# Row maxima in visits of seven, four banks to one reduction: an attention and MLP kernel on one core

## The chip, the core and the metric

The kernel runs on one core of a Trainium2 chip. The core has a matrix engine (TensorE, PE in the profile; its weight loads are PEld), a vector engine (VectorE, DVE), a scalar engine (ScalarE, ACT) and a general one (GpSimd, POOL). SyncE (SP) issues most of the transfers. Matmuls write to PSUM, which has eight banks of 512 fp32 columns by 128 partitions. The metric is the device time of one execution in microseconds.

## The reference

A token mixer with a gate: attention over 2048 tokens and a token-wise MLP on the same input, mixed by a sigmoid.

```
x = A_x                                  # 1 x 2048 x 448, fp32
g = sigmoid((x * gate_w).sum(-1))
q, k, v = split(x @ wqkv)                # 16 heads of 28
p = softmax(q k^T * 28**-0.5)
a = (p v) @ wo
y = layernorm(x)
b = gelu(y @ w1 + b1) @ w2 + b2          # 448 -> 1792 -> 448
out = g * a + (1 - g) * b
```

All of it is fp32. The kernel splits each operand of a product into a high and a low part and adds three products (high by high, high by low, low by high).

## The kernel before

The work runs in three stretches.

**Projections** (start to about 114 us). q, k and v of four chunks of 512 tokens are computed. q and k go out to DRAM (qk), v through three staging tiles `vt` to DRAM (vs). Each chunk has seven tiles of q and k and then four of v; a list `ahead`/`behind` with 44 steps (`at(step, ...)`) hangs loads, layer-norm statistics and the first weights of the MLP into this order. The pools of this stretch lie in SBUF where the MLP's tiles lie later: w2, then `hh` and `hl` in falling order of f. In the pool `qw` the tiles stand in this order: wh, wl, wv, then `vt`, then small ones, so that `vt` lies under `hh` and `hl` of f = 0 to 2.

**MLP** (about 114 to 467 us). Four chunks c, each with two phases. In the first, `mlp1(c, f)` runs 11 full-array matmuls for each of 14 blocks f into a PSUM bank, and ScalarE takes gelu of it twice (into `hh`, rounded, and `h`), GpSimd makes `hl`, the rest. In the second, `mlp2(c, i)` accumulates one of four token tiles i over the 14 blocks, three matmuls for each f, and ScalarE copies the sum out (`gb`). Both take banks 0 and 1 in turn, the very last tile bank 7. During the first chunk the weights w1 and w2 are still being loaded through staging tiles (s, lnr, more) and split.

**Attention** (about 467 us to the end). Scores of 16 pairs of four heads and 512 queries, exponentials on ScalarE, then products with v into bank 7. The softmax needs the maximum of each row of scores ahead of time, and these maxima are computed by extra matmuls of 28 rows, with one reduction on VectorE for each 512 keys.

**Row maxima.** This is what the change is about. `RowMax` holds 16 sets (four groups of heads by four query chunks) of 64 products each. A product is a 28-row matmul in one of the four row groups j of TensorE (line 440), for a query tile i and a key chunk k, into a bank; VectorE reduces it to one column of `mx` (lines 420 and 422). A 65th place per set, `close`, transposes the finished maxima (line 406). The next product is taken from the row group with most left, so that row groups follow each other 0, 1, 2, 3.

The sets are spread by `Filler` as filling work. In the MLP, `filler.run` is called after each matmul of the first phase and at two places for each f of the second. It counts `slot` up by the weight of that matmul and, once six products are due (MG), issues a visit of six on banks 2 to 7. Of the 1040 places 480 (MLP_MAX) are planned in the MLP; the remainder go singly into the attention loop, up to three at each group of five score units. When all are done the attention loop goes into a late mode with seven units to a group.

In `issue`, products that are held are reduced two banks at a time where the columns of `mx` allow; column (j * 4 + i) * 4 + k puts row groups 16 apart, and the pair is cut where j wraps from 3 to 0.

The order of each engine's work is written out by hand (`manual_schedule`), so instructions run in program order on each engine, and each waits by semaphores for what it needs.

Of the kernel before, what the change touches and what calls it, by code (L numbers as in the profile page):

```python
# [7 lines left out]
F32 = mybir.dt.float32  # L8
F32R = mybir.dt.float32r
AF = mybir.ActivationFunctionType  # L10
OP = mybir.AluOpType
AX = mybir.AxisListType.X
# [3 lines left out]
P = 128  # L16
S = 2048
D = 448
H = 16
# [6 lines left out]
TPC = CH // P  # L26
NF = F // P
NM = 2 * D // P
EPS = 1e-5
SCALE = DH ** -0.5  # L30
MLP_MAX = 480
MLP_G = MLP_MAX // 260
MG = 6
FS = 4
WARM = 10
W1, W2 = 0.233, 0.205
LINE = 16
LQ = 12
STEPS = (2, 5, 7, 8, 9, 10)
# [4 lines left out]
def kernel(ctx: ExitStack, tc: tile.TileContext, xt, wqk, wv, wo, xk, w1, b1, w2, b2,  # L44
                          ident_d, sel_d, out):
    nc = tc.nc
# [6 lines left out]
    eps_t = const.tile([P, 1], F32, name="eps_t")  # L53
# [22 lines left out]
    bank = ctx.enter_context(tc.tile_pool(name="pbank", bufs=1, space=PSUM)).tile([P, 8, CH], F32, name="bank")  # L76
# [80 lines left out]
    with tc.tile_pool(name="qx", bufs=2) as qx, tc.tile_pool(name="qo", bufs=4) as qo, \  # L157
# [11 lines left out]
        def spare(i):  # L169

            return mw1.tile([P, 2, CH], F32, name=f"w1f{i}")

        wh = qw.tile([P, NM, 4, P], F32R, name="wh")
        wl = qw.tile([P, NM, 4, P], F32R, name="wl")
        wt = {}
# [7 lines left out]
            nc.gpsimd.tensor_sub(wl[:, m], wt[m], wh[:, m].bitcast(F32))  # L183

        wvh, wvl = (qw.tile([P, 4, CH], F32R, name=f"wv{x}")[:, :, :450] for x in "hl")
        vt = [qw.tile([P, H, 32], F32, name=f"vt{i}") for i in range(3)]

        xh, xl = {}, {}
        xraw = {}
# [109 lines left out]
        banks = [next_ps() for m in range(NM)]  # L299
# [41 lines left out]
        def at(n, what, *args, to=behind):  # L341
            to[n].append((what, args))
# [13 lines left out]
        at(22, ln_turn, 0, TPC)  # L356
        at(24, ln_load, 0, to=ahead)
        at(28, ln_rows, TPC, NT)
        at(37, ln_turn, TPC, NT)
        for t, (f, x) in enumerate(((24, 27), (25, 28), (31, 34), (32, 35))):  # L360
            at(f, ln_fetch, 0, t, to=ahead)
# [19 lines left out]
    class RowMax:  # L381
# [27 lines left out]
            nc.vector.tensor_scalar(mt, ps[:4 * TPC, :P], -1.0, None, op0=OP.mult)  # L409
            self.queue.dma_start(ms[g][:, c * CH:(c + 1) * CH].rearrange("j (i x) -> j i x", x=P), mt.bitcast(F32))  # L410

        def issue(self, first, n, rows=None):

            held = []

            def reduce():
                if held:
                    (b0, c0), (b1, c1) = held[0], held[-1]
                    if b0 == b1:
                        nc.vector.reduce_max(self.mx[:, c0:c0 + 1], bank[:, b0], axis=AX)  # L420
                    else:
                        nc.vector.reduce_max(self.mx[:, c0:c1 + 1:c1 - c0], bank[:, b0:b1 + 1], axis=AX)  # L422
                    held.clear()

            for b in range(first, first + n):
                if self.done >= NG * NC * 65:
                    break
                self.done += 1
                left = sum(len(x) for x in self.left)
                if self.last is not None and (left <= 56 or self.n == NG * NC):  # L430
                    reduce()
                    self.close(bank[:, b])
                    continue
                most = max(range(4), key=lambda j: (len(self.left[j]), -j))
                j = max(rows, key=lambda j: len(self.left[j])) if rows else most
                if not self.left[j]:
                    j = most
                i, k = self.left[j].pop(0)
                r = slice(32 * j, 32 * j + DH)
                nc.tensor.matmul(bank[:, b], self.qds[self.n][r, i * P:(i + 1) * P],  # L440
                                 khi[self.n // NC][r, k * 512:(k + 1) * 512], start=True, stop=True)
                at = (j * TPC + i) * 4 + k
                if held and held[0][1] > at:
                    reduce()
                held.append((b, at))
                if len(held) == 2:
                    reduce()
                if left == 41 and self.n + 1 < NG * NC:
                    self.load(self.n + 1)
                g, c = divmod(self.n, NC)  # L450
                if c == NC - 1 and g < MLP_G and all(n != k for x in self.left for _, n in x):
                    load_khr(g + 1, k)
                if left == 1:
                    reduce()
                    self.last = mpool.tile([P, 4 * TPC], F32, name="mf")
                    nc.vector.reduce_max(self.last, self.mx.rearrange("p (a k) -> p a k", k=4), axis=AX)
                    if self.n + 1 < NG * NC:
                        self.begin(self.n + 1)
                    else:
                        self.n += 1  # L460
                        self.left = [[]] * 4
            reduce()

    class Filler:


        def __init__(self):
            self.max = None
            self.first = self.upto = self.slot = 0
            self.slots = 1  # L470

        @property
        def done(self):
# [10 lines left out]
            left = self.upto - self.done  # L484
            return left if self.slot >= self.slots else min(left, int(due))

        def run(self, n=1):


            if self.max is not None and self.due(n) >= min(MG, self.upto - self.done) > 0:  # L490
                self.max.issue(2, min(MG, self.upto - self.done))

    filler = Filler()

# [48 lines left out]
    def load_qm(n):  # L543

        while filler.done < min(65 * NG * NC, 65 * (n + 1) + 9):
            filler.max.issue(5, 1)
        g, c = divmod(n, NC)
        nc.sync.dma_start(qs[n][0][DH:P:32].bitcast(F32), ms[g][:, c * CH:(c + 1) * CH])

# [4 lines left out]
    def scores(units, most, tiles, between=None):  # L554

        def product(p, i):
            u = units[p]
            n, k, j = u // 4 // NT, u // 4 % NT, u % 4  # L560
            g, (qh, ql) = n // NC, qs[n]
            a, b, r = ((khi[g], qh, DH + 1), (klo[g], qh, DH), (khi[g], ql, DH))[i]
            r = slice(32 * j, 32 * j + r)
            nc.tensor.matmul(bank[:, p], a[r, k * P:(k + 1) * P], b[r], start=(i == 0), stop=(i == 2))  # L564

        def exps(at):
            t = tiles(len(at), at[0])
            nc.scalar.activation(t, bank[:, at[0]:at[-1] + 1], AF.Exp, scale=SCALE)  # L568
            for i, p in enumerate(at):
                probs[units[p]] = t[:, i]  # L570

        ua = len(units) - UA if len(units) > U else UA
        first, last = list(range(len(units)))[:ua], list(range(len(units)))[ua:]
        if most > 0:
            filler.max.issue(5, 1, [(units[0] + 3) % 4])
        for i in range(3):
            for p in first:
                product(p, i)
        exps(first)
        if between:  # L580
            between()
        for i in range(3):
            for p in last:
                product(p, i)
            if i == 0 and most > 1:
                filler.max.issue(6, 1, [(units[0] + 1) % 4, (units[0] + 2) % 4])
        if last:
            exps(last)
        if most > 2:
            filler.max.issue(5, 1, [(units[0] + 1) % 4, (units[0] + 2) % 4])  # L590


    ml = ExitStack()
# [7 lines left out]
    more = [mh.tile([P, CH], F32, name=f"more{i}") for i in range(2)]  # L601
# [4 lines left out]

    def mlp1(c, f):

        ps = bank[:, f % 2]
        ops = []  # L610
        for t in range(3):
            ops += [(w1h[f][:, t], yh[:, t]), (w1h[f][:, t], yl[:, t]), (w1l[f][:, t], yh[:, t])]
        ops += [(w1h[f][:, 3], yh[:, 3]), (w1l[f][:, 3], yh[:, 3])]
        for i, (a, b) in enumerate(ops):
            nc.tensor.matmul(ps, a, b, start=(i == 0), stop=(i == len(ops) - 1))  # L615
            filler.run(W1 if c else 0.65 * W1)
        h = mh.tile([P, CH], F32, name="h", bufs=2)
        nc.scalar.activation(hh[f], ps, AF.Gelu_apprx_tanh, bias=b1s[:, f:f + 1])  # L618
        nc.scalar.activation(h, ps, AF.Gelu_apprx_tanh, bias=b1s[:, f:f + 1])  # L619
        nc.gpsimd.tensor_sub(hl[f], h, hh[f].bitcast(F32))  # L620

    def mlp2(c, i):

        sl = slice(i * P, (i + 1) * P)
        last = c * TPC + i == NT - 1
        a = bank[:, 7 if last else i % 2, :D]
        for f in range(NF):
            nc.tensor.matmul(a, hh[f][:, sl], w2h[f], start=(f == 0), stop=False)  # L628
            nc.tensor.matmul(a, hh[f][:, sl], w2l[f], start=False, stop=False)  # L629
            rows = not last and (c * TPC + i < NT - 2 or f < 10) and (c + i > 0 or f > 3)  # L630
            if rows:
                filler.run(2 * W2)
            nc.tensor.matmul(a, hl[f][:, sl], w2h[f], start=False, stop=(f == NF - 1))  # L633
            if rows:
                filler.run(W2)
            if last and f == NF // 3:
                scores(list(range(U)), 0, early)
        gb = mh.tile([P, CH], F32, name="h", bufs=2)[:, :D]
        nc.scalar.activation(gb, a, AF.Copy)  # L639
        nc.sync.dma_start(gbs[c * TPC + i], gb)  # L640
# [199 lines left out]
    with tc.manual_schedule(engines=ENGINES):  # L840
# [3 lines left out]
        at = -1  # L844
# [124 lines left out]
```

## Time and profile before

| | |
|---|---|
| median of 3 runs | 1114.16 us (1113.55 to 1114.87) |
| the profiled execution | 1113.87 us, span 1112.1 us |
| TensorE busy | 1103.7 us (99%), 8156 matmuls, granted clock 1.000 |
| VectorE busy | 739.5 us (66%) |
| ScalarE busy | 634.4 us (57%) |
| GpSimd busy | 330.2 us (30%) |
| row-maxima reductions | 620 of one bank at 687 ns, 202 of two banks at 1219 ns |

A row of the timeline gives start, duration, engine, line, operation, what it writes and reads, and a count where like rows were merged; in square brackets stands idle time ahead of it and what ended that. Matmuls are pipelined: their rows overlap, so the distance from start to start is the time that one costs. A row of the windows view gives the stretch, its length, and busy time and count for each engine, then the granted clock, the share of the DMA engines and their GB/s. A group's row gives engine, operation, tiles, shapes and count, then busy time and mean, then idle time of the engine ahead of the group.

### The profile page before, as it was taken

To read this page: it belongs to the slowest core of one execution; us is meant where nothing else is said; L and a number is where in the kernel's file an instruction comes from. 1 tells how busy PE (TensorE), PEld (TensorE's weight loads), DVE (VectorE), ACT (ScalarE), POOL (GpSimd) and SP (SyncE) were. 2 spreads that over 40 slices of the span, in tenths; PEclk is the share of its full clock that TensorE was granted. 3 is DMA by queue.
4 is the path that set the end of the run, shared out by engine and by line. 5 is a ranking of instruction groups with operands and counts; after the bars stand their busy time and mean duration, and the time that the engine had idled before them with its cause. 6 is when DMAs were issued, how large, how long until landed. Compare 5 with 4: busy or idle time off the path is not lost.

```text
span 1112.1 us, 19809 instructions
## 1 busy us (share of the span) xinstructions
PE 1103.7 (99%) x8156; PEld 674.0 (61%) x8156; DVE 739.5 (66%) x1033; ACT 634.4 (57%) x660; POOL 330.2 (30%) x352
## 2 busy tenths in 40 slices
PE   9999999999999999999999999999999999999998
PEld 7888777777767767744444444444444444454546
DVE  3553488888888889576666676666667767747103
ACT  5434640331230231287877887887878878747572
POOL 5015564242334331013112221320223024343250
PEclk9999999999999999999999999999999999999999
DMA  7987641011111022162100220012011003002011
GB/s 258 356 272 277 178 125 49 9 47 39 47 55 37 25 65 75 49 165 74 28 19 20 61 73 20 20 28 52 27 58 37 18 20 94 12 26 69 35 53 59
DMA packets 53079, 84.35 MB, mean 76 GB/s; under 512 B 8516, under 2 KB 28500, under 8 KB 52076
## 3 DMA queue, kind: packets, MB, share of 16 engines
q1 hardware_dynamic: 48732, 76.27, 21.6%
q0 software_dynamic: 4256, 6.81, 2.3%
q8 instruction: 64, 1.05, 0.4%
q14 instruction: 27, 0.22, 0.1%
HBM read 56.40 MB, written 26.49 MB: 75 GB/s over the span
## 4 chain that ended last, share of the span: by engine, by line
PE 97%; DMA 1%; DVE 1%; ACT 1%; issue 0%; SPq 0%; ACTq 0%
PE bank L835 22%; PE bank L564 20%; PE bank L440 16%; PE bank L615 13%; PE bank L220 5%; PE bank L633 5%; PE bank L628 4%; PE bank L629 4%; PE bank L232 3%; PE bank L322 1%; PE bank L738 1%; PE bank L739 1%; PE bank L740 1%; DMA raw<-in_xt 1%; DMA vs<-vt 1%; DVE mx L420 0%
## 5 line engine op out<-in xcount | busy, mean ns | idle before, releaser
L568 ACT ACTIVATE pt<-bank 128x1536 f32<-128x1536 f32 (+1 forms) x387 | 461.5, 1243 | 122.0 <-PE bank L564 122.0
L420 DVE TENSOR_REDUCE mx<-bank 128x1 f32<-128x512 f32 x620 | 411.0, 687 | 173.6 <-PE bank L440 158.9
L835 PE MATMUL bank<-pt,vg 128*32 128x512 f32 x1948 | 260.4, 602 | 0.0
L422 DVE TENSOR_REDUCE mx<-bank 128x2 f32<-128x1024 f32 x202 | 237.7, 1219 | 32.0 <-PE bank L440 31.8
L440 PE MATMUL bank<-khi,qd 28*128 28x512 f32 x512 | 242.4, 480 | 0.3 <-DVE mx L420 0.2
L440 PEld LDWEIGHTS bank<-khi,qd 28*128 28x128 f32 x512 | 92.5, 181 | 150.1 <-DVE mx L420 107.8
L564 PE MATMUL bank<-qh,klo 28*128 28x512 f32 x1024 | 174.2, 392 | 0.0
L564 PE MATMUL bank<-qh,khi 29*128 29x512 f32 x768 | 156.4, 480 | 0.8 <-ACT khi L568 0.5
L615 PE MATMUL bank<-y,w1f 128*128 128x512 f32 x616 | 152.9, 398 | 0.3 <-ACT h L619 0.2
L615 PEld LDWEIGHTS bank<-y,w1f 128*128 128x128 f32 x616 | 112.4, 188 | 34.9 <-issue 11.8
L564 PE MATMUL bank<-ql,khi 28*128 28x512 f32 x768 | 129.9, 391 | 0.0
L620 POOL TENSOR_TENSOR hl<-h,hh 128x512 fp32r<-128x512 f32 x56 | 72.3, 1291 | 120.9 <-ACT h L619 74.0
L618 ACT ACTIVATE hh<-bank,b1s 128x512 fp32r<-128x512 f32 x56 | 38.5, 687 | 97.9 <-PE bank L615 96.2
L835 PEld LDWEIGHTS bank<-pt,vg 128*32 128x32 f32 x1948 | 44.6, 108 | 77.2 <-issue 76.8
L564 PEld LDWEIGHTS bank<-qh,klo 28*128 28x128 f32 x1024 | 87.4, 185 | 3.6
L756 POOL DMA_DIRECT2D lt<-ob x15 | 10.9, 724 | 255.7 <-DVE ob L755 255.7
L639 ACT ACTIVATE h<-bank 128x448 f32<-128x448 f32 x16 | 8.7, 544 | 135.1 <-PE bank L633 101.0
L564 PEld LDWEIGHTS bank<-qh,khi 29*128 29x128 f32 x768 | 60.9, 182 | 39.2 <-ACT pt L568 24.5
L633 PE MATMUL bank<-w2h,hl 128*128 128x448 f32 x224 | 84.6, 378 | 0.0
L628 PE MATMUL bank<-w2h,hh 128*128 128x448 f32 x224 | 83.1, 371 | 0.7 <-DVE mx L420 0.7
L629 PE MATMUL bank<-w2l,hh 128*128 128x448 f32 x224 | 81.4, 363 | 0.0
L440 PE MATMUL bank<-khr,qd 28*128 28x512 f32 x512 | 79.9, 466 | 0.0
(137 smaller groups left out, 1286.4 us busy)
## 6 DMA issues: line engine op xcount, KB each, us to landing
qk<-hl SPq DMA_DIRECT2D x28, 512.0 KB
raw<-in_xt SPq DMA_DIRECT2D x16, 256.0 KB
vs<-vt SPq DMA_DIRECT2D x16, 256.0 KB
s<-in_xt SPq DMA_DIRECT2D x16, 256.0 KB
rc<-rls POOLq DMA_DIRECT2D x60, 64.0 KB, 2.2
w1f<-in_xk SPq DMA_DIRECT2D x8, 448.0 KB
gbs<-h SPq DMA_DIRECT2D x16, 224.0 KB
klo<-qk SPq DMA_DIRECT2D x16, 224.0 KB
```

The source lines that it names most:

```text
L220: nc.tensor.matmul(ps, a, b, start=(i == 0), stop=(i == len(ops) - 1))
L420: nc.vector.reduce_max(self.mx[:, c0:c0 + 1], bank[:, b0], axis=AX)
L422: nc.vector.reduce_max(self.mx[:, c0:c1 + 1:c1 - c0], bank[:, b0:b1 + 1], axis=AX)
L440: nc.tensor.matmul(bank[:, b], self.qds[self.n][r, i * P:(i + 1) * P], khi[self.n // NC][r, k * 512:(k + 1) * 512], start=True, stop=True)
L564: nc.tensor.matmul(bank[:, p], a[r, k * P:(k + 1) * P], b[r], start=(i == 0), stop=(i == 2))
L568: nc.scalar.activation(t, bank[:, at[0]:at[-1] + 1], AF.Exp, scale=SCALE)
L615: nc.tensor.matmul(ps, a, b, start=(i == 0), stop=(i == len(ops) - 1))
L620: nc.gpsimd.tensor_sub(hl[f], h, hh[f].bitcast(F32))
L628: nc.tensor.matmul(a, hh[f][:, sl], w2h[f], start=(f == 0), stop=False)
L629: nc.tensor.matmul(a, hh[f][:, sl], w2l[f], start=False, stop=False)
L633: nc.tensor.matmul(a, hl[f][:, sl], w2h[f], start=False, stop=(f == NF - 1))
L835: nc.tensor.matmul(pv[32 * j:32 * j + 32, :], vg[n // NC][:, k, 32 * j:32 * j + 32], probs.pop(4 * step + j), start=(k == 0), stop=(k == N ...
```

## The change

Six edits:

- The accumulators of both MLP phases alternate between banks 0 and 7 in place of 0 and 1. Visits in the first phase use banks 1 to 6.
- In the second phase, for f from 2 to 9, a visit takes seven banks: 1 to 6 and whichever of 0 and 7 is not the accumulator of this tile. Outside these f, a visit has six and waits until eight products are due.
- `mx` has its columns in the order (k, i, j), so successive products are neighbours, and `reduce` joins held banks into one instruction where bank and column both go up by one, cut ahead of the fifth bank of the visit. A new rule, `clear`, holds the next visit until as many slots have gone by as the reductions of the last are reckoned to take (0.57 for each bank, less 0.5). The closing reduction of a set reads `mx` with a stride.
- MLP_MAX goes from 480 to 484; MG is dropped.
- A one-element gelu at step 30 of the projections loads ScalarE's table there.
- `vt` is allocated ahead of wh and wl, so it lies under `hh` and `hl` of the last f.

```diff
-MLP_MAX = 480
+MLP_MAX = 484
-MG = 6
+RED = 0.57
+        vt = [qw.tile([P, H, 32], F32, name=f"vt{i}") for i in range(3)]
         wh = qw.tile([P, NM, 4, P], F32R, name="wh")
...
-        vt = [qw.tile([P, H, 32], F32, name=f"vt{i}") for i in range(3)]
...
+        at(30, nc.scalar.activation, qw.tile([P, 1], F32, name="table"), eps_t, AF.Gelu_apprx_tanh)
...
             def reduce():
-                if held:
-                    (b0, c0), (b1, c1) = held[0], held[-1]
-                    if b0 == b1:
-                        nc.vector.reduce_max(self.mx[:, c0:c0 + 1], bank[:, b0], axis=AX)
-                    else:
-                        nc.vector.reduce_max(self.mx[:, c0:c1 + 1:c1 - c0], bank[:, b0:b1 + 1], axis=AX)
-                    held.clear()
+                while held:
+                    n = 1
+                    b, at = held[0]
+                    while n < len(held) and held[n] == (b + n, at + n) and held[n][0] not in banks[4:5]:
+                        n += 1
+                    nc.vector.reduce_max(self.mx[:, at:at + n], bank[:, b:b + n] if n > 1 else bank[:, b], axis=AX)
+                    del held[:n]
...
-                at = (j * TPC + i) * 4 + k
-                if held and held[0][1] > at:
-                    reduce()
-                held.append((b, at))
-                if len(held) == 2:
-                    reduce()
+                held.append((b, (k * TPC + i) * 4 + j))
...
-                    nc.vector.reduce_max(self.last, self.mx.rearrange("p (a k) -> p a k", k=4), axis=AX)
+                    nc.vector.reduce_max(self.last.rearrange("p (j i) -> p j i", j=4),
+                                         self.mx.rearrange("p (k i j) -> p j i k", k=4, j=4), axis=AX)
...
-        def run(self, n=1):
-            if self.max is not None and self.due(n) >= min(MG, self.upto - self.done) > 0:
-                self.max.issue(2, min(MG, self.upto - self.done))
+        def run(self, n=1, banks=(), wait=0):
+            if self.max is not None:
+                wait = 0 if banks else wait
+                banks = (banks or [1, 2, 3, 4, 5, 6])[:self.upto - self.done]
+                if self.due(n) >= min(len(banks) + wait, self.upto - self.done) > 0 and self.slot >= self.clear:
+                    self.max.issue(banks)
+                    self.clear = self.slot + len(banks) * RED - 0.5
...
-        ps = bank[:, f % 2]
+        ps = bank[:, 7 * (f % 2)]
...
-        a = bank[:, 7 if last else i % 2, :D]
+        a = bank[:, 7 * (i % 2), :D]
...
+            more = ([0, 1, 2, 3, 4, 5, 6] if i % 2 else [7, 1, 2, 3, 4, 5, 6]) if 2 <= f < NF - 4 else ()
             rows = not last and (c * TPC + i < NT - 2 or f < 10) and (c + i > 0 or f > 3)
             if rows:
-                filler.run(2 * W2)
+                filler.run(2 * W2, more, 2)
             nc.tensor.matmul(a, hl[f][:, sl], w2h[f], start=False, stop=(f == NF - 1))
             if rows:
-                filler.run(W2)
+                filler.run(W2, more, 2)
```

In the attention loop the calls `issue(5, 1, ...)` and `issue(6, 1, ...)` become `issue([5], ...)` and `issue([6], ...)`, with the same effect.

More of the change, by code (lines that the diff above doesn't have):

```diff
@@ L410, in close, with issue @@
             self.queue.dma_start(ms[g][:, c * CH:(c + 1) * CH].rearrange("j (i x) -> j i x", x=P), mt.bitcast(F32))
-        def issue(self, first, n, rows=None):
+        def issue(self, banks, rows=None):
             held = []
             def reduce():
-                if held:
-                    (b0, c0), (b1, c1) = held[0], held[-1]
-                    if b0 == b1:
-                        nc.vector.reduce_max(self.mx[:, c0:c0 + 1], bank[:, b0], axis=AX)
-                    else:
-                        nc.vector.reduce_max(self.mx[:, c0:c1 + 1:c1 - c0], bank[:, b0:b1 + 1], axis=AX)
-                    held.clear()
-            for b in range(first, first + n):
+                while held:
[5 more added lines that the diff above has]
+                    del held[:n]
+            for b in banks:
                 if self.done >= NG * NC * 65:
@@ L470, in __init__ @@
             self.slots = 1
+            self.clear = 0
         @property
@@ L545, in load_qm @@
         while filler.done < min(65 * NG * NC, 65 * (n + 1) + 9):
-            filler.max.issue(5, 1)
+            filler.max.issue([5])
         g, c = divmod(n, NC)
@@ L574, in scores @@
         if most > 0:
-            filler.max.issue(5, 1, [(units[0] + 3) % 4])
+            filler.max.issue([5], [(units[0] + 3) % 4])
         for i in range(3):
@@ L585, in scores @@
             if i == 0 and most > 1:
-                filler.max.issue(6, 1, [(units[0] + 1) % 4, (units[0] + 2) % 4])
+                filler.max.issue([6], [(units[0] + 1) % 4, (units[0] + 2) % 4])
         if last:
@@ L589, in scores @@
         if most > 2:
-            filler.max.issue(5, 1, [(units[0] + 1) % 4, (units[0] + 2) % 4])
+            filler.max.issue([5], [(units[0] + 1) % 4, (units[0] + 2) % 4])
     ml = ExitStack()
```

## The prediction

> **What bounds the kernel now.** I read the page first, then the chain that ended last, then TensorE's timeline inside single stages, and last VectorE and ScalarE beside it.
>
> ```profile
> PE 1103.7 (99%) x8156; PEld 674.0 (61%) x8156; DVE 739.5 (66%) x1033; ACT 634.4 (57%) x660; POOL 330.2 (30%) x352
> PEclk9999999999999999999999999999999999999999
> PE 97%; DMA 1%; DVE 1%; ACT 1%; issue 0%; SPq 0%; ACTq 0%
> L420 DVE TENSOR_REDUCE mx<-bank 128x1 f32<-128x512 f32 x620 | 411.0, 687 | 173.6 <-PE bank L440 158.9
> L422 DVE TENSOR_REDUCE mx<-bank 128x2 f32<-128x1024 f32 x202 | 237.7, 1219 | 32.0 <-PE bank L440 31.8
> ```
>
> TensorE is busy 99% of the span at full clock, and 97% of the chain is TensorE. So a change gains only what it takes out of TensorE's stream, or out of the few holes in it. The change works on the visits of the row maxima (line 440) inside the mlp stages. A visit is a handful of 28-row matmuls put between full-array ones. The second mlp phase has these (its four turns, in order; the last column pairs are matmul records of line 440):
>
> ```profile
> 154.40:197.60 43.20, 7.53 (x59) 3.41 (x59) 1.00 0.18 60
> 243.20:287.40 44.20, 8.39 (x65) 4.13 (x65) 1.00 0.12 40
> 332.50:376.60 44.10, 8.37 (x65) 4.03 (x65) 1.00 0.10 34
> 423.10:467.30 44.20, 6.19 (x47) 2.86 (x47) 1.00 0.11 37
> ```
>
> 59 + 65 + 65 + 47 = 236. Stepping the due rule of Filler.run through the loops gives 40 visits of six there (10, 11, 11, 8), or 240 places, four of which are the transposes of close. So code and trace agree, and the same stepping can be trusted for the changed rule.
>
> What does one visit cost? One piece of the second mlp phase, and the undisturbed pace at its end:
>
> ```profile
> 246.27 0.73 PE L440 MATMUL bank<-khr,qd 28*128 28x512 f32 x6
> 246.93 0.47 PE L633 MATMUL bank<-w2h,hl 128*128 128x448 f32 x1
> ...
> 250.16 0.73 PE L440 MATMUL bank<-khr,qd 28*128 28x512 f32 x6
> ...
> 456.95 0.47 PE L628 MATMUL bank<-w2h,hh 128*128 128x448 f32 x1 [0.72 <-DVE mx L420]
> 457.26 0.36 PE L629 MATMUL bank<-w2l,hh 128*128 128x448 f32 x1
> ...
> 459.88 0.37 PE L633 MATMUL bank<-w2h,hl 128*128 128x448 f32 x1
> ```
>
> From 457.26 to 459.88 lie 13 steps, so a full matmul takes 2.62 / 13 = 0.2015 us. From visit to visit (246.27 to 250.16, 3.89 us) lie 15 of them, 3.02 us. A visit of six costs 0.87 us of TensorE: two rounds (four row groups at once, then two) and the change of form on both sides. In the first phase:
>
> ```profile
> 114.31 5.19 PE L615 MATMUL bank<-y,w1f 128*128 128x512 f32 x22
> ...
> 301.49 0.82 PE L440 MATMUL bank<-khr,qd 28*128 28x512 f32 x6
> 302.24 3.21 PE L615 MATMUL bank<-y,w1f 128*128 128x512 f32 x13
> 305.38 0.73 PE L440 MATMUL bank<-khr,qd 28*128 28x512 f32 x6
> ```
>
> 22 in 5.19 us with the last 0.39 long give 0.2286 us each; 3.89 - 13 x 0.2286 = 0.92 us per visit.
>
> **Fewer visits.** Stepping the new rule (484 planned; seven in f 2 to 9, six elsewhere, wait 2 outside, clear) gives 41 visits of six in the first phase (was 40) and in the second 20 of seven and 16 of six (was 40 of six). That is 77 for 80; 482 of the 484 are issued and two slip into attention, because clear forbids one more call. Seven matmuls cycle over four row groups, so they still take two rounds, the second with three. That a second round of three starts together is seen in a score group:
>
> ```profile
> 1046.23 0.50 PE L564 MATMUL bank<-qh,khi 29*128 29x512 f32 x3
> 1046.57 0.39 PE L564 MATMUL bank<-qh,klo 28*128 28x512 f32 x3
> ```
>
> So the seventh is free, and the sum is -4 x 0.87 + 0.92 = **-2.6 us**. Bounds: -3.5 (the extra first-phase visit hidden in a hole) and +4.2 (each seventh opens a round of 1046.57 - 1046.23 = 0.34 us, 20 x 0.34 = 6.8). I take -2.6, nearest to the row just shown. Against it speaks a rule of the Trainium skill ("TensorE: Matmul & The Clock Gate", Part 3, the cost of the per-tile semaphore tail): semaphore increments of packed matmuls come one after the other, 26.3 ns each beside 4.7 ns per tile. By that page a seventh counting matmul would add, as an estimate, 31 ns to a visit, 20 x 31 ns = 0.6 us, and the whole sum below would be -3.2. No row here has seven, so the trace cannot yet say.
>
> **Reductions, and the banks they free.** Nothing of the kernel before shows three or four banks in one instruction. The two groups above give 1219 - 687 = 532 ns per further bank, so about 1.75 us for three and 2.28 for four. Back to back they overlap:
>
> ```profile
> 246.81 3.49 DVE L422 TENSOR_REDUCE mx<-bank 128x2 f32<-128x1024 f32 x3 [0.67 <-PE bank L440]
> 250.70 3.49 DVE L422 TENSOR_REDUCE mx<-bank 128x2 f32<-128x1024 f32 x3 [0.41 <-PE bank L440]
> ```
>
> Three pairs take 3.49, not 3.66: 0.08 saved per joint. The first starts 0.54 us after the visit. Before: the last pair is done 0.54 + 3.49 = 4.03 us after the visit, and the fifth matmul of the next visit, the first to need it, comes at 3.89 + 0.34 = 4.23. Margin 0.20. After, six as 4 + 2: 3.42, margin 0.27. Seven as 4 + 3 (odd tiles): 3.95; as 1 + 3 + 3 (even tiles, because bank 7 and bank 1 are not neighbours): 4.02, done at 4.56. The next visit after seven comes 18 matmuls on, 18 x 0.2015 + 0.87 = 4.50, its second round at 4.84. Margin 0.28. So no visit waits longer than now, and VectorE keeps its idle 0.4 us per visit. I book 0, bounds -1.5 (the small waits of visits beside a close go) and +2 (0.1 us in each of the 20 visits of seven). What was late next to DVE is the other accumulator: a visit of seven needs it copied out.
>
> ```profile
> 175.62 0.47 PE L633 MATMUL bank<-w2h,hl 128*128 128x448 f32 x1
> ...
> 176.19 0.54 ACT L639 ACTIVATE h<-bank 128x448 f32<-128x448 f32 x1 [10.02 <-PE bank L633]
> ```
>
> The copy is over 1.1 us after the last matmul of a tile; the earliest visit of seven (f = 2) comes eight matmuls, 1.6 us, later. Free.
>
> **The hole ahead of the last tile.** Now bank 7 is both a filler bank and the accumulator of the last tile. The last visit is at 452.81:
>
> ```profile
> 452.81 0.79 PE L440 MATMUL bank<-khr,qd 28*128 28x512 f32 x6
> ...
> 455.86 0.37 PE L633 MATMUL bank<-w2h,hl 128*128 128x448 f32 x1
> ...
> 456.21 0.68 DVE L420 TENSOR_REDUCE mx<-bank 128x1 f32<-128x512 f32 x1
> ```
>
> Bank 7 is reduced last (456.21 + 0.68 = 456.89), and the tile starts at 456.95. Its second matmul is at 457.26 where the pace gives 455.86 + 2 x 0.2015 = 456.26: a hole of 1.00 us. After the change the last visit is in tile 14 at f = 9 as well, but on banks 7, 1 to 6 with bank 7 reduced first, alone: free 0.54 + 0.69 = 1.23 us after the visit, with 13 matmuls (2.6 us) between. **-1.0 us**; bounds -1.0 and 0 (if something unseen holds the tile). The scores at f = 4 need banks 0 to 4, reduced by then (4.56 us against 13 + 14 matmuls, 5.4 us).
>
> **Gelu table and vt.** The third and fourth mlp1 rounds now start late:
>
> ```profile
> 117.08 1.28 ACT L618 ACT_TABLE_LOAD   x1 [1.98 <-PE bank L615]
> 118.37 0.69 ACT L618 ACTIVATE hh<-bank,b1s 128x512 fp32r<-128x512 f32 x1
> 118.96 0.68 ACT L619 ACTIVATE h<-bank,b1s 128x512 f32<-128x512 f32 x1
> 121.29 0.69 ACT L618 ACTIVATE hh<-bank,b1s 128x512 fp32r<-128x512 f32 x1 [1.65 <-DMA vs<-vt]
> ...
> 122.75 0.63 ACT L105 ACTIVATE w1f<-more 128x512 fp32r<-128x512 f32 x1 [0.19 <-DMA more<-in_w]
> ...
> 124.32 0.68 ACT L619 ACTIVATE h<-bank,b1s 128x512 f32<-128x512 f32 x1
> ...
> 119.69 3.65 PE L615 MATMUL bank<-y,w1f 128*128 128x512 f32 x13 [0.19 <-ACT h L619]
> ...
> 122.61 7.60 PE bank L615 x32
> 121.00:124.00 3.00, 2.87 (x13) 2.07 (x12) 0.59 (x1) 2.52 (x5) 1.31 (x2) 1.00 0.96 319
> ```
>
> Round 2 starts at 119.69 for 114.31 + 22 x 0.2286 = 119.34, round 3 at 122.61 for 119.69 + 2.51 = 122.20: 0.76 us lost. Both causes go: the table is loaded some 30 us earlier, where ScalarE has holes, and vt no longer lies under hh and hl of f = 0 to 2. But the next thing is late at once. ScalarE converts w1f from more before round 2's gelu, and that waits for its transfer, which lands just before 122.75 with the DMA engines 96% busy. So h of round 2 stays at 125.00, and round 4, which needs it, starts there instead of at about 125.2. **-0.15 us**, bounds 0 (the transfer lands even later) and -0.8 (it lands a microsecond earlier). The table's cover upstream:
>
> ```profile
> 90.33 0.60 ACT L208 ACTIVATE hl<-bank 128x512 fp32r<-128x512 f32 x1 [1.94 <-PE bank L220]
> ```
>
> 1.28 + 0.2 fit into idle stretches like this one's 1.94 us; without them TensorE would still have eight banks in turn. vt's new place lies under hh of the last f, written 30 us later. Its transfers and their order on SP's queue stay, as do the khr loads on POOL's.
>
> **Attention.** Two row maxima fewer there; stepping its loop gives 186 calls with three and none with two (was one), and 200 calls in all either way, so late mode starts one call sooner. **-0.1 us**, bounds -0.5 and +0.3 (late calls cut TensorE's stream once more). The strided read of mx at the end of a set stays one small instruction: 0.
>
> **Sum**: -2.6 - 1.0 - 0.15 - 0.1 = -3.85 us. The profiled execution took 1113.87 us, its span 1112.1; it would be 1110.0. The median of the runs, 1114.16, lies 0.3 above it: 1110.3.
>
> **Rivals.**
> *VectorE becomes the bound (slower).* If a four-bank instruction ran like four singles, 4 x 0.687 = 2.75 us, it would end 0.47 later; a visit of six then waits 0.47 - 0.27 = 0.20, one of seven (4 + 3, 0.78 more) about 0.45: 57 x 0.20 + 20 x 0.45 = 20 us, time 1131. It decides the sign from 3.85 / 77 = 0.05 us of wait per visit, that is from 0.32 us more reduction per visit. For it: VectorE is idle only 0.41 us per visit. Against: a pair costs less than two singles. Chance 0.07.
> *The seventh matmul costs a round (slower).* +6.8: time 1117. Against it the three-wide second round shown. Chance 0.05.
> *Visits of seven wait a little* (0.1 us each, 2 us): time 1112.3, about no change. For it margins of 0.2 to 0.3 us. Chance 0.12.
> *The hole at the last tile stays* because something else is late there: -2.85, time 1111.3. Nothing else is seen waiting. Chance 0.08.
> *More is won*: the transfer of w1f moves forward (-0.65 more) and the small waits beside closes go (-1): time 1108.7. Chance 0.13.
> The forecast itself, 1109.3 to 1111.5: 0.55.
>
> **The numbers.** 0.2% of this time is 2.2 us, about what a measurement here can tell from none. Faster by more: 0.55 + 0.13 + 0.08 = 0.76; the same 0.12; slower 0.12. The range goes from the wins of the last rival with a little beyond (1107.8) to the waits of seven at their worst (1114.0); it leaves out the two slower rivals and some tails.
>
> **What would show it.** 77 visits, 20 of them with seven, at 0.87 us from pace; four-bank reductions near 2.28 us; no TensorE idle with VectorE as releaser ahead of the last tile; no table load at the first gelu, and round 4 of mlp1 starting near 125.0. Wrong if fifth matmuls of a visit start late on VectorE, if the visit of seven is longer than that of six, or if early mlp1 gets new waits.

## The result, and the profile after

The changed kernel takes 1110.85 us (median of 8 runs, 1110.25 to 1111.74), the kernel before 1113.72 us in the same sessions. The ratio is 0.9974, with a 95% interval of 0.9963 to 0.9984: faster by 0.16% to 0.37%. Forecast were 1110.3 us and a gain of 3.85 us; measured are 2.87 us between the medians and 3.1 us between the spans of the two profiled executions (1112.1 and 1109.0).

The page of the changed kernel (busy time of the engines, the chain that ended last), and then its reductions by shape from the groups of instructions:

```profile
PE 1100.3 (99%) x8156; PEld 672.4 (61%) x8156; DVE 732.9 (66%) x932; ACT 634.3 (57%) x661; POOL 330.1 (30%) x352
PE 97%; DMA 1%; ACT 1%; DVE 0%; issue 0%; SPq 0%; ACTq 0%
```

```profile
L425 DVE TENSOR_REDUCE mx<-bank 128x1 f32<-128x512 f32 x568 | 375.3, 687 | 172.7 <-PE bank L443 158.7 <-PE bank L569 1.0
L425 DVE TENSOR_REDUCE mx<-bank 128x4 f32<-128x2048 f32 x58 | 132.9, 2291 | 32.0 <-PE bank L443 31.7
...
L425 DVE TENSOR_REDUCE mx<-bank 128x2 f32<-128x1024 f32 x61 | 73.9, 1214 | 0.6 <-PE bank L443 0.6
L425 DVE TENSOR_REDUCE mx<-bank 128x3 f32<-128x1536 f32 x34 | 58.5, 1747 | 0.4 <-PE bank L443 0.4
```

TensorE still carries the time. Four banks take 2291 ns and three 1747, where 2.28 and 1.75 us had been reckoned from singles and pairs.

Where did the 3.1 us go? Stage lengths, from the first matmul of a stage to the first of the next, in the two profiled executions:

| stage | before | after | difference |
|---|---|---|---|
| projections | 114.31 | 114.16 | -0.15 |
| first phases, four chunks | 40.31, 45.82, 45.37, 46.72 | 40.69, 46.02, 46.28, 45.98 | +0.75 |
| second phases, four chunks | 42.91, 43.94, 43.88, 44.21 | 42.15, 43.24, 43.49, 42.37 | -3.69 |
| attention, to the last matmul | 640.36 | 640.32 | 0.0 |

The time from the start to the first MLP matmul scatters over 0.9 us between the profiled executions of all kernels here (113.37 to 114.31), so -0.15 says nothing. The first phases hold one visit more (41 for 40). The gain is in the second phases. Their records of row-maxima matmuls (windows view, line 443 alone; the matmul count is the first one in brackets):

```profile
154.85:197.00 42.15, 6.89 (x58) 3.01 (x58) 1.00 0.19 60
243.02:286.26 43.24, 7.82 (x65) 3.51 (x65) 1.00 0.12 40
332.55:376.04 43.49, 8.11 (x64) 3.58 (x64) 1.00 0.11 34
422.01:464.38 42.37, 5.47 (x45) 2.34 (x45) 1.00 0.12 38
```

58 + 65 + 64 + 45 = 232, which is 20 x 7 + 16 x 6 less four transposes: the 36 visits that the due rule gave on paper. One visit of seven in TensorE's timeline, and the next visit 18 matmuls on:

```profile
245.34 0.74 PE L443 MATMUL bank<-khr,qd 28*128 28x512 f32 x7
246.00 0.47 PE L640 MATMUL bank<-w2h,hl 128*128 128x448 f32 x1
...
249.84 0.74 PE L443 MATMUL bank<-khr,qd 28*128 28x512 f32 x7
```

From visit to visit (245.34 to 249.84) lie 4.50 us and 18 full matmuls. 4.50 - 18 x 0.2015 = 0.87 us, the price of a visit of six. The seventh matmul is free.

VectorE beside it, a visit of seven (4 + 3) and one of six (4 + 2):

```profile
258.87 3.95 DVE L425 TENSOR_REDUCE mx<-bank 128x4 f32<-128x2048 f32 x2 [0.48 <-PE bank L443]
263.41 3.42 DVE L425 TENSOR_REDUCE mx<-bank 128x4 f32<-128x2048 f32 x2 [0.59 <-PE bank L443]
```

Both are the reckoned lengths, and VectorE still sits idle about half a microsecond ahead of each of the two.

The hole ahead of the last tile is gone (TensorE's timeline; the last matmul of tile 14, then the first two of tile 15):

```profile
453.78 0.36 PE L640 MATMUL bank<-w2h,hl 128*128 128x448 f32 x1
453.98 0.37 PE L633 MATMUL bank<-w2h,hh 128*128 128x448 f32 x1
454.19 0.36 PE L634 MATMUL bank<-w2l,hh 128*128 128x448 f32 x1
```

What was not forecast stands at two places. The first is the start of the MLP (TensorE, then ScalarE):

```profile
114.16 10.18 PE L620 MATMUL bank<-y,w1f 128*128 128x512 f32 x44
125.34 1.42 PE L620 MATMUL bank<-y,w1f 128*128 128x512 f32 x5 [1.01 <-ACT h L624]
```

```profile
119.38 0.69 ACT L623 ACTIVATE hh<-bank,b1s 128x512 fp32r<-128x512 f32 x1 [1.23 <-PE bank L620]
119.97 0.68 ACT L624 ACTIVATE h<-bank,b1s 128x512 f32<-128x512 f32 x1
123.03 0.63 ACT L105 ACTIVATE w1f<-more 128x512 fp32r<-128x512 f32 x1 [2.39 <-DMA more<-in_w]
123.57 0.56 ACT L115 ACTIVATE w2h<-s 128x448 fp32r<-128x448 f32 x1
124.04 0.67 ACT L623 ACTIVATE hh<-bank,b1s 128x512 fp32r<-128x512 f32 x1
124.61 0.67 ACT L624 ACTIVATE h<-bank,b1s 128x512 f32<-128x512 f32 x1
```

Rounds 0 to 3 now run without a break (44 matmuls in 10.18 us), and then round 4 (each round is one block f, 11 matmuls) waits a whole microsecond for the gelu of round 2, which stands behind the conversion of w1f. That waited 2.39 us for its transfer.

The second is the visit that holds the transpose of close (line 408). Here it is the second of seven places:

```profile
271.15 0.50 PE L443 MATMUL bank<-khr,qd 28*128 28x512 f32 x1
271.58 0.28 PE L408 MATMUL bank<-ident,mf 128*16 128x128 f32 x1
271.79 0.73 PE L443 MATMUL bank<-khr,qd 28*128 28x512 f32 x5
272.44 0.47 PE L640 MATMUL bank<-w2h,hl 128*128 128x448 f32 x1
```

From the visit's start to the next full matmul lie 1.29 us, where an ordinary visit takes 0.66. The full-array transpose splits the visit: one matmul alone in the array, then the transpose, then two more rounds.

To weigh this over all visits, I take for each the time from the full matmul ahead of it to the second one behind it, less 1.315 us in the first phase and 1.266 in the second (what an undisturbed visit takes there). A sum of this excess over the MLP tells what waits and splits cost:

| kernel | visits with a transpose (7) | all others |
|---|---|---|
| before | 1.83 us | 1.89 us |
| changed | 2.81 us | 1.22 us |

So the transposes took back 0.98 us, and the ordinary visits gave 0.67. Of the 0.98, 0.45 stands at the two transposes that now cut a visit of seven: 0.62 and 0.65 us, where the same two cost 0.41 each in a visit of six. The other 0.53 comes from the places at which the transposes fell in visits of six; one that stood first and cost 0.10 now stands third and costs 0.41.

### The profile page after: what moved, and what is told of

It reads as the page before. It is cut to its first block, busy times and chain, and to the rows that moved or that the text cites. A ratio compares the mean times of both kernels' runs of the same rounds, so it can differ in the third digit from the quotient of the medians.

```text
span 1109.0 us, 19711 instructions
## 1 busy us (share of the span) xinstructions
PE 1100.3 (99%) x8156; PEld 672.4 (61%) x8156; DVE 732.9 (66%) x932; ACT 634.3 (57%) x661; POOL 330.1 (30%) x352
## 4 chain that ended last, share of the span: by engine, by line
PE 97%; DMA 1%; ACT 1%; DVE 0%; issue 0%; SPq 0%; ACTq 0%
PE bank L842 22%; PE bank L569 20%; PE bank L443 16%; PE bank L620 13%; PE bank L221 5%; PE bank L640 5%; PE bank L633 4%; PE bank L634 4%; PE bank L233 3%; PE bank L323 1%; PE bank L745 1%; PE bank L746 1%; PE bank L747 1%; DMA raw<-in_xt 1%; DMA more<-in_w 1%
## 5 line engine op out<-in xcount | busy, mean ns | idle before, releaser
L425 DVE TENSOR_REDUCE mx<-bank 128x1 f32<-128x512 f32 (+3 forms) x721 | 634.7, 911 | 205.8 <-PE bank L443 191.4
L443 PE MATMUL bank<-khr,qd 28*128 28x512 f32 x512 | 76.8, 462 | 0.0
L569 PEld LDWEIGHTS bank<-ql,khi 28*128 28x128 f32 x768 | 65.6, 185 | 11.7
```

The source lines that it names most:

```text
L425: nc.vector.reduce_max(self.mx[:, at:at + n], bank[:, b:b + n] if n > 1 else bank[:, b], axis=AX)
```

## The experiments

The theory from these two traces: the second phases gain 0.87 us per visit saved and the hole; the table and vt only move a wait; the transposes, cut into longer visits, give part of the gain back. The rivals: the edits at the MLP's start cost something; VectorE's joined reductions carry the gain; the number of visits is worth less than 0.87 us each. The runs below were taken in three later sessions. The kernel before has medians of 1113.88 to 1114.0 us in these, for 1113.72 above, so medians of different sessions compare to about 0.3 us, and smaller differences are read from the stages.

**The table and vt undone.**

```diff
-        vt = [...]                       # ahead of wh
+        vt = [...]                       # behind wv
-        at(30, nc.scalar.activation, qw.tile([P, 1], F32, name="table"), eps_t, AF.Gelu_apprx_tanh)
```

> The changed kernel without the early gelu table and with vt back in its old place. Theory (the two edits only move the wait: round 4 of mlp1 waits for gelu of round 2, which stands behind the transfer of w1f): within 0.4 us of the changed kernel, about 1110.9; rounds 2 and 3 late again by 0.76 us in all, round 4 without a wait, starting at about 125.2. Rival (the edits win what they were booked for at the most): 0.8 us slower than the changed kernel, 1111.6. Second rival (the edits cost, because the first chunk's first phase went from 40.31 to 40.69 us): 0.4 us faster, 1110.4.

Measured: 1111.72 us (1110.9 to 1112.95), 0.87 slower than the changed kernel. But the first phase of the first chunk is 40.51 us, not longer than the 40.69 of the changed kernel: rounds 2 and 3 are late again, and round 4 starts without a wait.

```profile
114.14 5.19 PE L619 MATMUL bank<-y,w1f 128*128 128x512 f32 x22
119.52 2.79 PE L619 MATMUL bank<-y,w1f 128*128 128x512 f32 x11 [0.19 <-ACT h L623]
122.63 4.17 PE L619 MATMUL bank<-y,w1f 128*128 128x512 f32 x17 [0.32 <-ACT h L623]
```

Round 4 follows at 125.26, 11.12 us after the phase's start; in the changed kernel 11.18. So the rival that they win their 0.8 us there falls, although the total seemed to speak for it. The second rival, that they cost 0.4 us, is not borne out either: 0.18 us between two executions is within the scatter of this stage. The loss is elsewhere: attention took 641.81 us for 640.32. Five exponentials, at 562.1, 657.0, 751.4, 846.6 and 941.0 us, start 0.32 us behind the semaphore instruction that releases them, where others start 0.045 us behind it. So they are 0.28 us late, and TensorE loses close to 0.3 us at each. The first of them in ScalarE's timeline:

```profile
559.13 2.37 ACT L572 ACTIVATE pt<-bank 128x1536 f32<-128x1536 f32 x2 [1.19 <-PE bank L568]
562.11 2.37 ACT L572 ACTIVATE pt<-bank 128x1536 f32<-128x1536 f32 x2 [0.61 <-PE bank L442]
```

**One small copy in the gelu's place.** Does that come from vt and the table, or from the length of ScalarE's program?

```diff
+        at(30, nc.scalar.activation, qw.tile([P, 1], F32, name="table"), eps_t, AF.Copy)   # on the kernel above
```

> The kernel without the early table and with vt in its old place, with one small copy on ScalarE at step 30 instead of the gelu, so that ScalarE's program has about the length of the changed kernel's. Theory (without that instruction five exponentials 94 us apart started 0.32 us late in the attention, because of where they fall in ScalarE's program): none of the five is late, attention 640.3 us instead of 641.8, time about 1110.6. Rival (the late starts come from the table or from vt's place): they stay, 1111.7.

Measured: 1110.67 us (1110.18 to 1112.43), attention 640.46 us, none of the five late. The same place of ScalarE's timeline:

```profile
559.07 2.37 ACT L573 ACTIVATE pt<-bank 128x1536 f32<-128x1536 f32 x2 [1.19 <-PE bank L569]
561.76 2.37 ACT L573 ACTIVATE pt<-bank 128x1536 f32<-128x1536 f32 x2 [0.33 <-PE bank L569]
```

The gelu table is loaded late in this kernel and vt lies in its old place, and it is as fast as the changed kernel. So these two edits are worth nothing here, and the loss came with one instruction less on ScalarE.

The records say more about these five. Counted with the semaphore instructions, exactly 128 recorded instructions of ScalarE lie from one late start to the next, and 0.6 to 1.0 us after each of them a packet of 8 KB comes in on the queue that carries instructions. The first of these packets, in the DMA view of 560 to 565 us:

```profile
q14 instruction: 1, 0.01, 0.6%
```

In the changed kernel and in the run with the copy the instruction at the same counts is an exponential that queues behind another, or a semaphore wait, and none of the five is late. So the late starts go with the fetching of ScalarE's program, and cost time only where the first instruction of a block of 128 is one that TensorE will wait for. No run changes the fetching itself, so this last step is argued.

**Visits of six everywhere.**

```diff
-            more = ([0, 1, 2, 3, 4, 5, 6] if i % 2 else [7, 1, 2, 3, 4, 5, 6]) if 2 <= f < NF - 4 else ()
+            more = ()
-                filler.run(2 * W2, more, 2)      # and filler.run(W2, more, 2)
+                filler.run(2 * W2)
```

> The changed kernel with visits of six everywhere (banks 1 to 6, accumulators still on 0 and 7, joined reductions kept). Theory (a visit costs 0.87 us whatever it holds, and seven saves about four of them): second phases longer by 2.6 to 3.5 us in all, time about 1113.7 to 1114.2; no hole ahead of the last tile, since bank 7 is no filler bank. Rival (the gain is in the reductions or the banks, not in the number of visits): the time stays at 1110.9.

Measured: 1112.83 us (1112.21 to 1114.92), 1.98 slower than the changed kernel. The second phases have 39 visits and take 172.86 us in all, 1.61 more. Both the theory's 2.6 and the rival's zero are missed there. Three visits at 0.87 are 2.6 us; the excess at transposes is 2.20 us here for 2.81, and at the other visits 0.86 for 1.22, so 0.97 us came back over the whole MLP. Attention, which is left two more products (480 instead of 482 are issued in the MLP), takes 641.10 us for 640.32, so not all of the 1.98 is the visits'.

**At most two banks to a reduction.**

```diff
-                    while n < len(held) and held[n] == (b + n, at + n) and held[n][0] not in banks[4:5]:
+                    while n < len(held) and held[n] == (b + n, at + n) and held[n][0] not in banks[4:5] and n < 2:
```

> The changed kernel with at most two banks to a reduction. Theory (VectorE has a margin of 0.2 to 0.3 us per visit, and pairs lengthen a visit of seven by 0.15 us and one of six by 0.07): no wait at ordinary visits, time within 0.4 us of the changed kernel, 1110.9. Rival (joined reductions carry the gain, VectorE is the bound of a visit): waits of 0.1 us or more at most visits, 77 x 0.1 = 8 us, time about 1118.

Measured: 1110.91 us (1110.38 to 1111.29), no difference in the total. The stages show one: the first phase of the first chunk is 0.48 us shorter in this execution (40.21 for 40.69; the transfer of w1f came sooner), and the seven MLP stages behind it are 0.51 us longer. The excess of ordinary visits is 1.70 us for 1.22. So the margin of VectorE is real, but joining three and four banks is worth about 0.5 us; it is not what wins the rest.

**One bank to a reduction.**

```diff
+ ... and n < 1:      # in the same line
```

> The changed kernel with every reduction of one bank. Theory (a reduction ends in time with a margin of 0.2 to 0.3 us; singles follow each other at about 0.60 us, so a visit of six is done 0.54 + 3.69 = 4.23 us after its start and one of seven after 4.83, against 4.23 and 4.84 when they are needed): the margin is just used up, waits of 0 to 0.1 us per visit, and more at the ends of sets; time 1111 to 1116, and the waits stand at the fifth matmul of the visits. Rival (VectorE has more in hand than reckoned): 1110.9.

Measured: 1115.39 us (1114.92 to 1117.82), 4.5 slower than the changed kernel and slower than the kernel before (ratio 1.0016, 1.0007 to 1.0025). The excess of ordinary visits rises from 1.22 to 6.0 us, mostly in steps of 0.1 to 0.2 at each visit. Six singles of a visit in VectorE's timeline, then two visits in TensorE's, which now take 0.77 and 0.84 us instead of 0.66, and the weight loads of these two:

```profile
207.39 3.68 DVE L425 TENSOR_REDUCE mx<-bank 128x1 f32<-128x512 f32 x6 [0.25 <-PE bank L443]
```

```profile
210.78 0.84 PE L443 MATMUL bank<-khr,qd 28*128 28x512 f32 x6
211.55 3.28 PE L620 MATMUL bank<-y,w1f 128*128 128x512 f32 x13
...
218.62 0.90 PE L443 MATMUL bank<-khr,qd 28*128 28x512 f32 x6
219.46 0.74 PE L620 MATMUL bank<-y,w1f 128*128 128x512 f32 x2
```

```profile
210.78 0.53 PEld L443 LDWEIGHTS bank<-khr,qd 28*128 28x128 f32 x6 [0.35 <-DVE mx L425]
...
218.62 0.59 PEld L443 LDWEIGHTS bank<-khr,qd 28*128 28x128 f32 x6 [0.35 <-DVE mx L425]
```

The wait stands at the last matmul of a visit, not at the fifth as expected: its weights are loaded only when VectorE has reduced the last bank of the visit before. In the 54 visits whose last weight load comes over 0.2 us behind the first matmul the excess sums to 5.95 us, in the other 16 to 0.05. The forecast's rival of a VectorE that ends late is thus no fancy: it costs 4.8 us where the reductions of a visit grow from 3.42 to 3.68 us, and 0.5 us with the pairs of the run before.

**Conversions behind the gelus.** If round 4 waits only because of the order on ScalarE, another order should set the gain free.

```diff
-                    for k in stage(f):
-                        high(k)
...
                 mlp1(c, f)
+                if c == 0:
+                    for k in stage(f):
+                        high(k)
```

> The changed kernel with the conversions of w1 and w2 on ScalarE moved behind the two gelus of the same round in the first chunk. Theory (round 4 of mlp1 waits 1.1 us only because gelu of round 2 stands behind the conversion that waits for its transfer): round 4 starts at about 124.2 instead of 125.3 and the gain stays, time about 1109.8. Rival (a later round then waits for its weights, or gelu for the next conversion): round 4 early, but the first phase as long as before, time 1110.9.

Measured: 1109.44 us (1109.02 to 1111.22), 1.41 faster than the changed kernel; the first phase of the first chunk takes 39.39 us for 40.69. TensorE runs 56 matmuls without a wait:

```profile
113.87 12.90 PE L620 MATMUL bank<-y,w1f 128*128 128x512 f32 x56
```

**The same order on the kernel before.** The diff is the same.

> The kernel before, with only the conversions moved behind the gelus as in the run with that edit on the changed kernel. Theory (the table load and the transfers from vt still delay rounds 2 and 3 by 0.76 us, and round 4 was not late there): the first phase of the first chunk stays within 0.3 us of 40.3 us, time 1113.7 to 1114.0. Rival (that order alone was worth the 1.3 us and the table and vt nothing): first phase 39.4 us, time about 1112.7.

Measured: 1114.7 us (1113.74 to 1116.27), ratio to before 1.0008 (0.9999 to 1.0016): no gain. Rounds 2 and 3 are late:

```profile
119.22 2.79 PE L615 MATMUL bank<-y,w1f 128*128 128x512 f32 x11 [0.66 <-ACT h L619]
122.44 3.94 PE L615 MATMUL bank<-y,w1f 128*128 128x512 f32 x16 [0.43 <-ACT h L619]
```

The theory had the first phase within 0.3 us of 40.3; it took 41.05, and the second phase behind it 43.38 for 42.91, with all its visits counted as before. The rival's 39.4 us did not come. So the early table and vt alone gain nothing, nor does the order alone, and together they gain 1.3 us in that phase: there are two waits in a row, and both must go. No run tells the table from vt here.

**Bank 7 reduced last ahead of the last tile.**

```diff
+            if more and c * TPC + i == NT - 2:
+                more = [1, 2, 3, 4, 5, 6, 7]
```

> The changed kernel, with the banks of the visits in the last tile but one in the order 1 to 7, so that bank 7 is reduced in the last instruction of a visit and not in the first. Theory (the hole of 1.0 us ahead of the last tile was the wait for the reduction of bank 7): a hole of 1.0 to 1.2 us is back at that place, time about 1112.0. Rival (the hole went because the last visit lies one matmul earlier or for another reason): no hole, 1110.9.

Measured: 1111.85 us (1111.19 to 1112.95), 1.0 slower than the changed kernel. The hole is back:

```profile
453.23 0.37 PE L642 MATMUL bank<-w2h,hl 128*128 128x448 f32 x1
454.61 0.47 PE L633 MATMUL bank<-w2h,hh 128*128 128x448 f32 x1 [1.01 <-DVE mx L425]
454.92 0.37 PE L634 MATMUL bank<-w2l,hh 128*128 128x448 f32 x1
```

454.92 - 453.23 - 2 x 0.2015 = 1.29 us. The order in which banks are reduced decides it, and the rival, another reason for the lost hole, falls.

**The transpose first in its visit.**

```diff
-                if self.last is not None and (left <= 56 or self.n == NG * NC):
+                if self.last is not None and (left <= 56 and b == banks[0] or self.n == NG * NC):
```

> The changed kernel, with the transpose that closes a set held back until it is the first of a visit. Theory (in the changed kernel the seven visits with a transpose cost 2.8 us more than others, because it cuts the visit in two and brings TensorE's change of form twice more; in first place it costs 0.1): 1.5 to 2.1 us less in the MLP, time about 1109.0. Rival (the cost is the wait for VectorE's closing reduction, wherever the transpose stands): the seven visits cost as much as before, time 1110.9.

Measured: 1109.13 us (1108.25 to 1109.78), 1.72 faster than the changed kernel. The excess at the seven transposes falls from 2.81 to 0.74 us, 0.1 each. One of them:

```profile
275.57 0.27 PE L408 MATMUL bank<-ident,mf 128*16 128x128 f32 x1
275.77 0.51 PE L443 MATMUL bank<-khr,qd 28*128 28x512 f32 x4
```

In first place the transpose follows a full-array matmul and no longer cuts the visit in two; the rival, that the wait for VectorE's closing reduction is what costs, falls. The other visits' excess rises to 2.05 us: six visits that follow a closing reduction wait 0.17 to 0.37 us. By the excess the gain is thus 1.24 us, not 1.72; the profiled execution, the slowest of the five, has 1.0 us in its span.

**All three together**: conversions behind the gelus, the transpose first, and the closing reduction of a set issued behind the other reductions of its visit.

```diff
-                    nc.vector.reduce_max(self.last.rearrange(...), self.mx.rearrange(...), axis=AX)
+                    ended = self.mx
...
             reduce()
+            if ended is not None:
+                nc.vector.reduce_max(self.last.rearrange(...), ended.rearrange(...), axis=AX)
```

> Three edits on the changed kernel together: conversions behind the gelus, the transpose first in its visit, and VectorE's closing reduction behind the other reductions of its visit. Theory: -1.4 (conversions, measured alone), -1.5 to -2.1 (transpose), -0.5 (five waits of 0.1 to 0.3 us in the visit behind a closing reduction shrink to half): time about 1107.2. Rival (these holes give way to one another): no better than 1109.4, the time with the conversions alone.

Measured: 1106.53 us (1106.19 to 1107.1), ratio to the kernel before 0.9931 (0.9919 to 0.9944). The excess is 0.72 us at transposes and 0.45 elsewhere, so the waits behind closing reductions are gone, and the first phase of the first chunk takes 39.39 us. None of the three gives way to another. It beats both kernels: 0.7% faster than before, and 4.3 us faster than the changed one.

**Six everywhere on that kernel.** The edit of the run with six, on the kernel with the three further edits.

> The kernel with the three further edits, with visits of six everywhere. Theory (three or four visits at 0.87 us, and nothing given back at the transposes any more): second phases longer by 2.6 to 3.5 us than with seven (169.38 us), time about 1109.1 to 1110. Rival (seven is worth no more than the 1.6 us seen in the second phases of the changed kernel): 1108.1.

Measured: 1109.75 us (1109.49 to 1111.88), 3.2 slower; second phases 172.60 us for 169.38, again with 39 visits of six for 36. With the transposes out of the way, seven is worth the 2.6 us of three visits. The 0.6 us above that is excess: one visit of the first chunk waits 0.84 us in this run. That settles the gap left by the first run with six.

## Why the prediction was right, and where its terms were off

The median lies inside the range, the change went the way that was forecast, and its size is three quarters of the forecast one.

- *Fewer visits, -2.6*: right. 77 visits and their split came from the code, the price of 0.87 us from the trace, and the run with six on the cleaned kernel shows it. The seventh matmul cost nothing, not 0.34 us: by the rows, a visit of seven and one of six both cost 0.87 us. The 31 ns of the semaphore rule that was set against it ("TensorE: Matmul & The Clock Gate" in the Trainium skill, Part 3, the per-tile semaphore tail) are not seen either. In the run with one bank to a reduction all matmuls of a visit count up a semaphore, and the two visits of six and of seven at 164.6 and 159.7 us, which wait for nothing, both have an excess of 0.005 us.
- *Reductions, booked at 0*: the lengths were right to 0.01 us, and the ordinary visits wait less than before, not more. The step that failed is "I book 0": it left out the transposes. One of them breaks a visit of seven into three rounds where it left a visit of six in two (0.45 us for the two such visits), and the new stepping moved the others to other places of their visits (0.53). By the excess, transposes cost 0.98 us more and the others 0.67 less, +0.3 in all. Where a transpose falls in its visit was not worked out ahead, so the 0.53 could as well have gone the other way.
- *The hole, -1.0*: right, and right for the reason given; reducing bank 7 last brings it back.
- *Gelu table and vt, -0.15*: the mechanism was right and was forecast word for word (round 4 waits for a transfer that does not come sooner). The size was off: the conversion that waits for the transfer started 0.3 us later (0.4 counted from the phase's start), and the phase grew by 0.38. Round 4's start lies 10.7 to 11.7 us after the phase's start in six profiled executions with the two edits, and 10.95 to 11.27 in three without, all with the conversions in their old order. So no gain is seen, the scatter is about half a microsecond, and the bound of 0 was too narrow. This part of the miss is scatter; whether the edits make the transfer later is open.
- *Attention, -0.1*: 0.0.

Together: -2.6 + 0.3 - 1.0 + 0.4 - 0.15 (the start of the program) = -3.05, against the 3.1 us between the spans. The two terms that carry the forecast, visits and hole, hold each by a run of its own; what is missing is the 0.3 of the transposes and the 0.4 of the transfer.

Of the rivals, the VectorE bound did not come, but lies close: 0.26 us more reduction per visit costs 4.8 us in all, where the forecast had 0.27 to 0.28 of margin, and 0.07 already costs 0.5. The forecast put the first wait at the fifth matmul; it stands at the last. "More is won" named the two right places, the transfer behind w1f and the waits beside closes; only they were not won by this change but by the three further edits.

## What to carry to other kernels

When filling work costs a fixed price per visit (here 0.87 us for six matmuls as for seven), count visits and not work, and see that nothing of another form stands in the middle of one. A wait that is removed is worth what the next wait behind it leaves: look for that one first, and move it in the same edit. When two versions differ by 0.1%, compare stages and not totals: a single instruction more or less can move a loop that no one touched, and a transfer that lands early can hide a loss.

## What was not expected of the hardware

- Five ScalarE instructions, about 94 us and exactly 128 instructions apart in a loop that is the same in all kernels, started 0.28 us late in the changed kernel without the one-element instruction at step 30. They were not late with it, and not in the kernel before, which has no such instruction but a different number ahead of the loop. The cost was 1.4 us in attention.
- A full-array transpose of 128 columns costs 0.1 us at the head of a visit of row-group matmuls and 0.4 to 0.65 us inside one.
- Six or seven row-group matmuls that all count up a semaphore hold up the matmul behind them no longer than those of which two or three do: the excess is 0.005 us where nothing else waits.
